# Spreading an attention stage's row scatters over its steps, one behind each step's softmax sum

## The chip, the cores and the metric

The kernel runs on one core of a Trainium2 chip. The metric is the device time of one execution in microseconds (us). The engines are named as in the profile: PE (TensorE), PEld (its weight loads), DVE (VectorE), ACT (ScalarE), POOL (GpSimd) and SP (SyncE, which here only issues DMAs). Each engine works through its own instructions in the order in which the program gives them; engines wait for each other by semaphores.

## What is computed

Three layers, one behind the other, in float32. Only what matters here stands below.

```python
def _attn_ref(q, k, v, n_global, n_local):          # q, k, v: 2 x 8 x 768 x 64
    scores = scale * np.matmul(q, k.transpose(0, 1, 3, 2)) + bias
    scores = np.where(is_global | is_local, scores, -1000000000.0)
    a = np.exp(scores - np.max(scores, axis=-1, keepdims=True))
    a = a / (np.sum(a, axis=-1, keepdims=True) + 1e-09)
    return np.matmul(a, v)

def _moe_ref(x, w_gate, w_noise, noise, w1, w2):     # x: 1536 tokens x 512, 8 experts
    noisy_logits = x @ w_gate + np.log1p(np.exp(x @ w_noise)) * noise
    top2 = np.argpartition(-noisy_logits, 2, axis=1)[:, :2]
    ...
    for e in range(E):
        ...
            h = np.maximum(x[mask] @ w1[e], 0.0)
            out[mask] += top2_w[mask, k, None] * (h @ w2[e])

def _moe2_ref(x, w_in, w_out):
    h = x @ w_in
    g = h * (1.0 / (1.0 + np.exp(-h)))
    return (g @ w_out).astype(np.float32)
```

## The kernel before, in words

The 1536 tokens are 12 tiles of 128 (6 for each batch). **The attention stage** is one loop over steps s = 0 to 50 (line 715). Step s belongs to tile n = s // 4 and to the pair of heads c = s % 4. It has a small software pipeline: `scores(s)` (line 503) is two score matmuls on PE, one for each head of the pair, and a DVE operation on each that adds the bias and takes the minimum (line 516); `expo(s)` (line 519) is the exponential of both on ACT, whose running sum goes into a column of `SM[n]` (line 526). Two steps later `p_t` transposes the result on PE into a bank of PSUM and copies it out on ACT (lines 535 and 537), three steps later `av` multiplies it with the values (line 547). So PE, DVE and ACT hand small pieces of work to each other several times in a step. Around this the loop hangs the preparation of the next tile (lines 486 to 501), the normalising of the tile before (`post`, line 554, whose row factor is the small DVE operation at line 556), loads (lines 382 to 392 on SP), and at c = 3 of tiles 2 to 7 a split of a weight block into two float32r parts on POOL (`split_high`, `split_low`, lines 317 and 324).

**Routing** (`route`, line 603) runs for groups of tiles: tiles 0 to 3, 4 to 7, 8 and 9, 10 and 11. It is a generator that the loop advances piece by piece. It finds the two experts of every token and the row that the token gets in a buffer `XS` in HBM (448 rows for each expert), and then scatters the normalised tiles there, each tile twice (j = 0 for its first expert's row, j = 1 for its second's), by an indirect DMA of 128 rows that POOL issues (line 642). By the order of the generator, the scatters of the first group are issued in step 26, those of the second in step 42, those of the third in step 50; those of the last group come in the expert stage. Between the j = 0 and the j = 1 scatters of the second group, SP's queue gets the loads of expert 0's first two blocks from `XS` (`load_x`, line 687). `reads` is the list of such loads, `scats` that of the scatters; the lists serve to tell the framework that they touch different rows.

**The expert stage** (line 1052 on) and the last layer follow. They are long chains of matmuls on PE (lines 788 to 852), with weights that stream in through SP's queue as buffers come free.

Of the kernel before, what the change touches and what calls it, by code (L numbers as in the profile page):

```python
# [9 lines left out]
F32 = mybir.dt.float32  # L10
# [10 lines left out]
P = 128  # L21
# [9 lines left out]
def fr(t):  # L31
    return t.bitcast(F32)


def noisy_logits(nc, tl, L, nz, lg, fine=False):


    co = (2.0000000078777487, 0.6666631593508026, 0.40024853723499904, 0.27961418834331303, 0.2817465726538725)
    E = lg.shape[-1]
    z = L[:, :, E:]  # L40
    a, b, s2, pl = tl("ta", E), tl("tb", E), tl("tc", E), tl("td", E)
    nc.scalar.activation(a, z, AF.Abs)
    nc.scalar.activation(a, a, AF.Tanh, scale=0.5)
    yield
    nc.vector.tensor_scalar(b, a, 3.0, None, op0=OP.add)
    nc.vector.reciprocal(b, b)
    if fine:
        yield
    nc.vector.tensor_scalar(a, b, 4.0, -1.0, op0=OP.mult, op1=OP.add)
    nc.vector.tensor_tensor(s2, a, a, op=OP.mult)  # L50
    if fine:
        yield
    nc.vector.tensor_scalar(pl, s2, co[4], None, op0=OP.mult)
    for kk in (3, 2, 1):
        nc.vector.scalar_tensor_tensor(pl, pl, co[kk], s2, op0=OP.add, op1=OP.mult)
        if fine and kk != 2:
            yield
    nc.vector.scalar_tensor_tensor(pl, pl, co[0], a, op0=OP.add, op1=OP.mult)
    yield
    nc.vector.scalar_tensor_tensor(pl, z, 0.0, pl, op0=OP.max, op1=OP.add)  # L60
    nc.vector.tensor_tensor(lg, pl, nz, op=OP.mult)
    nc.vector.tensor_tensor(lg, lg, L[:, :, :E], op=OP.add)
# [188 lines left out]
def attn_moe_mlp(ctx, tc, q, k, v, n_global, n_local, w_gate, w_noise, noise,  # L251
                 w1, w2, w_in, w_out, out):
    nc = tc.nc
# [5 lines left out]
    HP = H // 2  # L259
# [5 lines left out]
    XR = E * CAP  # L265
# [12 lines left out]
    xnp = xctx.enter_context(tc.tile_pool(name="xnp", bufs=1))  # L278

    XS = dram.tile([XR, DM], F32, name="XS")  # L280
# [40 lines left out]
    def split_low(k, pool):  # L321
        u, part = divmod(k, 2)
        hi, lo = unit[u][2 * part:2 * part + 2]
        (nc.gpsimd if pool else nc.vector).tensor_tensor(lo, raw[k], fr(hi), op=OP.subtract)  # L324
# [16 lines left out]
    slots = xnp.tile([P, NT, 2], I32, name="slots")  # L341
# [139 lines left out]
    QH, SB, PN, MN, SM, PT, OT, XT, XN = {}, {}, {}, {}, {}, {}, {}, {}, {}  # L481
# [37 lines left out]
    def expo(s):  # L519
        n, c = divmod(s, HP)  # L520
        wd = WK if tiles[n][1] else P
        if c == 0:
            SM[n] = xnp.tile([P, H], F32, name="sm", bufs=3)
        PN[s] = awk.tile([P, 2, WK], F32, name="pn", bufs=3)
        for j in range(2):
            nc.scalar.activation(PN[s][:, j, :wd], SB[s][:, j, :wd], AF.Exp, bias=MN[s][:, j:j + 1], scale=-1.0,  # L526
                                 accum_out=SM[n][:, 2 * c + j:2 * c + j + 1])
# [69 lines left out]
    T0, T1 = 8, 2  # L597
# [3 lines left out]
    scats, fills, reads = [], [], []  # L601

    def route(t0, t1, psum, fine=False):
        m = t1 - t0
        g = slice(t0, t1)

        def tl(nm, *sh):
            return xnp.tile([P, GM, *sh], F32, name=nm)[:, :m]

        lg, sel, lu, lh = lgs[:, g], sels[:, g], lus[:, g], slh[:, g]  # L610
        yield from noisy_logits(nc, tl, L[:, g], nz[:, g, :], lg, fine)
        if fine:
            yield
        top = tl("top", 8)
        for t in range(t0, t1):
            nc.vector.max(top[:, t - t0], lgs[:, t])
        nc.vector.tensor_tensor(sel, lg, top[:, :, 1:2].to_broadcast([P, m, E]), op=OP.is_ge)
        if fine:
            yield
        yield  # L620
        pos = psum()[:, :m * E].rearrange("p (t e) -> p t e", e=E)
        nc.tensor.matmul(pos, tri, sel, start=True, stop=False)
        for s in range(1, m):
            nc.tensor.matmul(pos[:, s:], ones, sel[:, :m - s], start=False, stop=False)
        nc.tensor.matmul(pos, ones, selcum[:, None, :].to_broadcast([P, m, E]), start=False, stop=True)
        un, s3 = tl("un", E), tl("s3", E)
        nc.vector.tensor_scalar(un, sel, BIG2, -BIG2, op0=OP.mult, op1=OP.add)
        if not fine:
            yield
        nc.vector.tensor_tensor(s3, pos, eover[:, None, :].to_broadcast([P, m, E]), op=OP.is_ge)  # L630
        nc.vector.scalar_tensor_tensor(s3, s3, BIG, pos, op0=OP.mult, op1=OP.add)
        if fine:
            yield
        nc.vector.tensor_tensor(lh[:, :, 0], un, s3, op=OP.subtract)
        nc.vector.tensor_tensor(lh[:, :, 1], sel, s3, op=OP.mult)
        if fine:
            yield
        nc.vector.tensor_reduce(lu, lh, axis=AX.X, op=OP.max)
        nc.vector.tensor_tensor(slots[:, g, :], lu, sgn[:, None, :].to_broadcast([P, m, 2]), op=OP.mult)
        for j in range(2):  # L640
            for t in range(t0, t1):
                st = nc.gpsimd.indirect_dma_start(
                    out=XS[:, :], out_offset=bass.IndirectOffsetOnAxis(ap=slots[:, t, j:j + 1], axis=0),
                    in_=XN[t], in_offset=None, bounds_check=XR - 1, oob_is_err=False)
                for o in scats + (reads if j else []):
                    tc.declare_no_dep(st.ins, o.ins, reason="rows of other slots")
                scats.append(st)
            if j == 0 and t1 in (T0, NT):
                for t in ((0, 1) if t1 == T0 else (2, 3)):
                    load_x(0, t)  # L650
        yield
        cs = xnp.tile([P, E], F32, name="cs")
        nc.vector.tensor_reduce(cs, sel.rearrange("p t e -> p e t"), axis=AX.X, op=OP.add)
        nc.vector.tensor_tensor(selcum, selcum, cs, op=OP.add)
        if t1 == T0:
            nc.vector.tensor_copy(chk[:, E + 1:E + 2], selcum[:, 0:1])
# [30 lines left out]
    def load_x(e, t):  # L687
        XE[e, t] = (xnp if e == 0 else mx_).tile([P, DM], F32, name="xe", bufs=4)
        a, b = blk[e][t]
        ld = (nc.gpsimd if e == 0 and t > 1 else nc.sync).dma_start(XE[e, t][:b - a], XS[e * CAP + a:e * CAP + b, :])  # L690
        reads.append(ld)

    routing, later = [], []
    R1, R2 = (0,1,1,1), (1,2,0,2)
    NS = NT * HP

    def start(g):
        if next(g, g) is not g:
            later.append(g)

    def routed(k):
        for _ in range(k):
            if routing and next(routing[0], routing) is routing:
                routing.pop(0)

    def prep(c):
        for g in prep_q(0, c, c + 2), prep_k(0, c, c + 2, c == 0):
            for _ in g:
                pass
# [5 lines left out]
    for s in range(NS + 3):  # L715
        n, c = divmod(s, HP)
        if s < NS:
            scores(s)
            expo(s)
        if s == 0:  # L720
            prep(HP // 2)
        later = [g for g in later if next(g, g) is not g]
        routed(R1[c])
        if 2 <= s < NS + 2:
            p_t(s - 2)
        if 3 <= s < NS + 3:
            av(s - 3)
        if c == 0:
            later = [g for g in later if next(g, g) is not g]
        routed(R2[c])  # L730
        if n < NT:
            if c == 0 and 2 <= n + 2 < NT:
                load_qk(n + 2)
                load_v(n + 2)
            if c == 1 and n + 1 < NT:
                start(prep_q(n + 1))
            if c == 2 and n + 1 < NT:
                start(prep_k(n + 1))
            if s == 1:
                late_consts()  # L740
            if s == 2:
                load_small()
            if s == 6:
                zero_fill()
        if c == 3 and n >= 1:
            start(post(n - 1, tbank))
        if c == 0 and n >= 2 and n - 2 in groups:
            routing.append(route(*groups[n - 2], tbank, True))
        if c == 1 and 2 <= n <= 10:
            load_half(n - 2)  # L750
        if c == 3 and 2 <= n <= 7:
            split_high(n - 2, True)
            split_low(n - 2, True)
    for g in later + routing:
        for _ in g:
            pass
# [295 lines left out]
    for i, (e, f, tm, ts) in enumerate(steps):  # L1052
# [23 lines left out]
        s = slice(blk[e][ts[0]][0], blk[e][ts[-1]][1])  # L1076
# [3 lines left out]
        n = s.stop - s.start if e < E - 1 else HC  # L1080
# [112 lines left out]
    for gr, f in todo:  # L1193
# [10 lines left out]
        if gr + 1 < len(GS):  # L1204
            t, m = tok[gr + 1], GS[gr + 1]
            a, odd = divmod(f - (G0 if gr == 0 else 2), 2)
# [39 lines left out]
```

## Time and profile before

| | |
|---|---|
| median of 3 runs | 757.39 us (755.98 to 757.83) |
| profiled execution | 757.51 us |
| its span, first to last instruction | 755.6 us |
| outside the span | 1.9 us |
| PE busy | 724.7 us (96%) |
| DVE busy | 454.1 us (60%) |
| ACT busy | 271.9 us (36%) |
| POOL busy | 192.2 us (25%) |
| mean granted TensorE clock | 0.990 |

The profile is of one execution. Times in it count from the first instruction. The attention stage fills about the first 135 us, the expert stage the stretch from there to about 500 us, the last layer the rest. In the timeline, a row is one instruction or several alike: start, duration, engine, line, operation, the tiles that it writes and reads, the form, the count; in brackets the idle time of the engine before it and who ended that. The ends of matmuls are modelled. The end of a scatter's row is the end of what POOL does for it, not the landing of its data.

### The profile page before, as it was taken

The numbers are of one execution on the slowest core, as the hardware profiler recorded it, in microseconds if no ns is written. First come the engines' busy times: TensorE is split into PE (matmuls) and PEld (weight loads), VectorE is DVE, ScalarE is ACT, GpSimd is POOL, SyncE is SP. The second block draws the span as 40 slices with busy tenths as digits, with TensorE's granted clock in tenths as the row PEclk, the third lists the DMA queues.
The fourth block names the chain that finished last, engine by engine and source line by source line (L and its number), as shares of the span: only waits on it lengthen the run. The fifth ranks groups of instructions, "written<-read, shape, count | busy, mean of one in ns | idle before, by whom it ended". The sixth has DMA issues, their size and how long they took to land.

```text
span 755.6 us, 11279 instructions
## 1 busy us (share of the span) xinstructions
PE 724.7 (96%) x4055; PEld 596.5 (79%) x4055; DVE 454.1 (60%) x991; ACT 271.9 (36%) x635; POOL 192.2 (25%) x178
## 2 busy tenths in 40 slices
PE   8997897998998999999999999999999999999996
PEld 4665565897887787888888888888888888888995
DVE  4668574747888898887888874674233332322332
ACT  5665574334343443433333454452112111111110
POOL 4134503345443333353434221422011000000000
PEclk9999997999999999999999999999999999999999
DMA  8866755258868578686868743752012010000101
GB/s 161 203 151 147 220 153 187 84 175 245 284 215 295 172 248 259 208 272 201 275 217 265 240 169 125 239 167 72 28 29 56 14 57 1 0 1 1 57 0 33
DMA packets 96431, 111.93 MB, mean 148 GB/s; under 512 B 36495, under 2 KB 65999, under 8 KB 96360
## 3 DMA queue, kind: packets, MB, share of 16 engines
q1 hardware_dynamic: 89096, 94.37, 41.7%
q0 software_dynamic: 6608, 16.10, 6.5%
q8 instruction: 43, 0.70, 0.4%
q10 hardware_dynamic: 656, 0.53, 0.2%
q14 instruction: 28, 0.23, 0.1%
HBM read 84.00 MB, written 32.51 MB: 154 GB/s over the span
## 4 chain that ended last, share of the span: by engine, by line
PE 61%; DVE 3%; issue 2%; DMA 1%; ACT 0%; POOL 0%; POOLq 0%; ACTq 0%
PE h L788 10%; PE h L789 10%; PE h L791 10%; PE y L837 9%; PE y L841 9%; PE y L842 9%; PE tp L770 2%; PE y L851 1%; PE y L852 1%; DVE ct L903 1%; DMA yu<-YS,gidx 0%; POOL co L909 0%; DMA YS<-ye 0%; DVE ct L906 0%; DVE co L908 0%
## 5 line engine op out<-in xcount | busy, mean ns | idle before, releaser
L788 PE MATMUL h<-xh,u1h 128*128 128x256 f32 (+4 forms) x544 | 181.4, 345 | 2.6 <-DVE h L1061 2.5
L789 PE MATMUL h<-xh,u1l 128*128 128x256 f32 (+4 forms) x544 | 178.1, 339 | 0.0
L841 PE MATMUL y<-u2h,hx 128*128 128x512 f32 x368 | 145.4, 395 | 1.0 <-ACT hx L814 1.0
L842 PE MATMUL y<-u2l,hx 128*128 128x512 f32 x368 | 145.1, 394 | 0.0
L1146 DVE CAST hx<-h 128x256 fp32r<-128x256 f32 (+1 forms) x64 | 35.7, 558 | 153.4 <-ACT h L1145 152.4
L791 PE MATMUL h<-xl,u1h 128*128 128x256 f32 (+4 forms) x544 | 118.2, 339 | 0.0
L837 PE MATMUL y<-u2h,hx 128*128 128x512 f32 x368 | 109.3, 396 | 6.6 <-DVE hx L815 6.6
L788 PEld LDWEIGHTS h<-xh,u1h 128*128 128x128 f32 x544 | 102.5, 188 | 14.1 <-DVE h L1061 2.9
L789 PEld LDWEIGHTS h<-xh,u1l 128*128 128x128 f32 x544 | 102.6, 189 | 10.2
L791 PEld LDWEIGHTS h<-xl,u1h 128*128 128x128 f32 x544 | 91.7, 188 | 8.2
L1145 ACT ACTIVATE h<-h 128x256 f32<-128x256 f32 (+1 forms) x64 | 30.4, 475 | 183.0 <-PE h L791 182.9
L837 PEld LDWEIGHTS y<-u2h,hx 128*128 128x128 f32 x368 | 68.8, 188 | 24.6 <-DVE hx L815 9.3
L909 POOL TENSOR_TENSOR co<-ct,co 128x512 f32<-128x512 f32 x32 | 41.3, 1289 | 167.2 <-issue 128.9
L841 PEld LDWEIGHTS y<-u2h,hx 128*128 128x128 f32 x368 | 69.2, 188 | 13.8 <-ACT hx L814 1.2
L842 PEld LDWEIGHTS y<-u2l,hx 128*128 128x128 f32 x368 | 69.2, 188 | 12.4
L1084 ACT ACTIVATE hx<-h 128x64 fp32r<-128x64 f32 x64 | 14.3, 224 | 143.1 <-DVE hx L815 143.1
L526 ACT ACTIVATE pn<-sb,mn 128x232 f32<-128x232 f32 (+1 forms) x96 | 44.8, 467 | 42.0 <-DVE mn L516 37.0
L773 DVE TENSOR_TENSOR xl<-tp,xh 128x512 fp32r<-128x512 f32 (+1 forms) x44 | 28.1, 642 | 39.5 <-ACT xh L772 39.5
L815 DVE SCALAR_TENSOR_TENSOR hx<-h,hx 128x448 fp32r<-128x448 f32 (+2 forms) x72 | 38.7, 537 | 20.7 <-ACT hx L814 19.1
L814 ACT ACTIVATE hx<-h 128x448 fp32r<-128x448 f32 (+2 forms) x72 | 34.7, 482 | 34.5 <-PE h L791 31.1
L324 POOL TENSOR_TENSOR u1l<-ra,u1h 128x1024 fp32r<-128x1024 f32 x16 | 41.4, 2587 | 6.1 <-ACT u1h L319 5.8
L319 ACT CAST u1h<-ra 128x1024 fp32r<-128x1024 f32 x37 | 38.9, 1052 | 5.4 <-DMA ra<-WI 4.1
(226 smaller groups left out, 1046.2 us busy)
## 6 DMA issues: line engine op xcount, KB each, us to landing
ra<-in_moe_w SPq DMA_DIRECT2D x32, 512.0 KB
rb<-in_moe_w SPq DMA_DIRECT2D x32, 512.0 KB
cx<-in_moe_w_in SPq DMA_DIRECT2D x16, 512.0 KB
cx<-in_moe_w_out SPq DMA_DIRECT2D x16, 512.0 KB
xe<-XS SPq DMA_DIRECT2D x22, 256.0 KB
YS<-yx SPq DMA_DIRECT2D x18, 256.0 KB
WI<-co SPq DMA_DIRECT2D x16, 256.0 KB
WO<-co SPq DMA_DIRECT2D x16, 256.0 KB
```

The costliest lines, as they stand in the source:

```text
L319: nc.scalar.copy(hi, raw[k])
L324: (nc.gpsimd if pool else nc.vector).tensor_tensor(lo, raw[k], fr(hi), op=OP.subtract)
L526: nc.scalar.activation(PN[s][:, j, :wd], SB[s][:, j, :wd], AF.Exp, bias=MN[s][:, j:j + 1], scale=-1.0, accum_out=SM[n][:, 2 * c + j:2 * c ...
L788: nc.tensor.matmul(p, a, xh[:, c, s], start=(c == 0), stop=False)
L789: nc.tensor.matmul(p, b, xh[:, c, s], start=False, stop=False)
L791: nc.tensor.matmul(p, wh[:, c, o:o + P], xl[:, c, s], start=False, stop=(c == NC - 1))
L815: nc.vector.scalar_tensor_tensor(hl, p, 0.0, fr(hh), op0=OP.max, op1=OP.subtract)
L837: nc.tensor.matmul(PY[t][:s.stop - s.start], hl[:, s], uh[:, a, :], start=False, stop=(f == nf - 1))
L841: nc.tensor.matmul(PY[t][:s.stop - s.start], hh[:, s], uh[:, a, :], start=(f == 0), stop=False)
L842: nc.tensor.matmul(PY[t][:s.stop - s.start], hh[:, s], ul[:, a, :], start=False, stop=False)
L909: nc.gpsimd.tensor_tensor(o, a, o, op=OP.add)
L1146: nc.vector.tensor_copy(hh, p)
```

## The change

In the steps of the attention stage a new function `leave(s)` is called behind `expo(s)`. If scatters are pending, it puts a copy of one column of the step's softmax sums to a one-column tile `paced` onto POOL's queue, and behind it one pending scatter. The scatters of the first group (eight: both j of tiles 0 to 3) and the j = 1 scatters of the second group (four) are put on the pending list where they were issued before; all others are issued where they were. What is pending behind the loop's end would be issued there. So the first group's scatters go to steps 27 to 34, the second group's four j = 1 scatters to steps 43 to 46, and the second group's j = 0 scatters stay four in a row in step 42.

```diff
+        def scatter(t, j):
+            st = nc.gpsimd.indirect_dma_start(
+                out=XS[:, :], out_offset=bass.IndirectOffsetOnAxis(ap=slots[:, t, j:j + 1], axis=0),
+                in_=XN[t], in_offset=None, bounds_check=XR - 1, oob_is_err=False)
+            for o in scats + (reads if j else []):
+                tc.declare_no_dep(st.ins, o.ins, reason="rows of other slots")
+            scats.append(st)
+
         for j in range(2):
             for t in range(t0, t1):
-                st = nc.gpsimd.indirect_dma_start(
-                    ...
-                scats.append(st)
+                if t1 < T0 or t1 == T0 and j:
+                    pend.append((scatter, t, j))
+                else:
+                    scatter(t, j)
...
+    pend = []
+    paced = xnp.tile([P, 1], F32, name="paced")
+
+    def leave(s):
+        n, c = divmod(s, HP)
+        if pend:
+            nc.gpsimd.tensor_copy(paced, SM[n][:, 2 * c:2 * c + 1])
+            fn, *a = pend.pop(0)
+            fn(*a)
+
...
             scores(s)
             expo(s)
+            leave(s)
...
+    for fn, *a in pend:
+        fn(*a)
```

## Rows read from the trace of the kernel before

**Rows 1.** Windows: length, busy us of each engine (count), granted clock, DMA share, GB/s.
```profile
112.20:123.70 11.50, 7.53 (x56) 4.77 (x54) 4.10 (x17) 3.29 (x12) 7.84 (x8) 0.79 0.59 203
124.00:129.60 5.60, 5.25 (x29) 3.30 (x30) 3.65 (x18) 3.67 (x13) 0.00 (x0) 0.54 0.52 192
160.00:180.00 20.00, 20.00 (x136) 17.93 (x135) 12.93 (x24) 8.55 (x16) 8.85 (x7) 1.00 0.86 265
```

**Rows 2.** Timeline, PE: first score matmul of steps 32, 35 and 36.
```profile
85.92 0.46 PE L511 MATMUL h<-kth,qh 64*128 64x232 f32 x1
...
92.83 0.46 PE L511 MATMUL h<-kth,qh 64*128 64x232 f32 x1
...
95.68 0.46 PE L511 MATMUL h<-kth,qh 64*128 64x232 f32 x1
```

**Rows 3.** Timeline, PE: first score matmul of steps 28 and 44 to 47.
```profile
72.33 0.46 PE L511 MATMUL h<-kth,qh 64*128 64x232 f32 x1
...
115.27 0.46 PE L511 MATMUL h<-kth,qh 64*128 64x232 f32 x1
...
120.55 0.75 PE L511 MATMUL h<-kth,qh 64*128 64x232 f32 x1
...
125.40 0.75 PE L511 MATMUL h<-kth,qh 64*128 64x232 f32 x1
...
128.57 0.75 PE L511 MATMUL h<-kth,qh 64*128 64x232 f32 x1
```

**Rows 4.** Timeline, POOL: scatters that begin, and within the second run, end a run.
```profile
69.88 1.25 POOL L642 DMA_INDIRECT XS<-xn,slots  x1 [1.75 <-DVE slots L639]
...
112.17 1.07 POOL L642 DMA_INDIRECT XS<-xn,slots  x1 [19.67 <-DVE slots L639]
...
116.09 0.97 POOL L642 DMA_INDIRECT XS<-xn,slots  x1 [0.31 <-issue]
...
121.20 0.97 POOL L642 DMA_INDIRECT XS<-xn,slots  x1 [0.30 <-issue]
135.73 0.97 POOL L642 DMA_INDIRECT XS<-xn,slots  x1 [13.55 <-DVE slots L639]
...
147.74 0.97 POOL L642 DMA_INDIRECT XS<-xn,slots  x1 [7.20 <-DVE hx L815]
```

**Rows 5.** Timeline: what PE finished inside the runs of eight, and its readers.
```profile
115.86 0.70 PE L535 MATMUL tp<-ident,pn 128*116 128x128 f32 x4
119.41 0.40 DVE L516 CUSTOM_DVE_ANT_0 sb<-y,bias 128x232 f32<-128x232 f32 x1 [0.91 <-remote]
...
123.71 0.58 ACT L537 COPY pts<-tp 116x512 f32<-116x512 f32 x1 [3.27 <-PE y L535]
...
81.66 0.60 ACT L489 ACTIVATE qh<-y 128x512 f32<-128x512 f32 x1 [1.06 <-PE y L547]
```

**Rows 6.** Timeline: PE and its reader ACT beside a run of four, beside two scatters.
```profile
138.37 0.61 PE L791 MATMUL h<-xl,u1h 128*128 128x192 f32 x4
...
140.04 0.33 ACT L814 ACTIVATE hx<-h 128x192 fp32r<-128x192 f32 x1 [0.83 <-PE h L791]
...
147.79 0.61 PE L791 MATMUL h<-xl,u1h 128*128 128x192 f32 x4
...
148.49 0.33 ACT L814 ACTIVATE hx<-h 128x192 fp32r<-128x192 f32 x1 [0.51 <-PE h L791]
```

**Rows 7.** Timeline: a POOL split, and small DVE work beside it and beside a scatter.
```profile
64.66 1.05 POOL L317 TENSOR_SCALAR u2h<-rb 128x1024 fp32r<-128x1024 f32 x1 [6.88 <-DMA rb<-in_moe_w]
65.79 2.35 POOL L324 TENSOR_TENSOR u2l<-rb,u2h 128x1024 fp32r<-128x1024 f32 x1
65.99 2.18 DVE L627 TENSOR_SCALAR un<-sels 128x32 f32<-128x32 bf16 x1
...
70.29 0.68 DVE L498 COPY kth<-tp 128x512 f32<-128x512 f32 x1
```

**Rows 8.** Timeline, ACT: the exponential of step 44's first head.
```profile
118.54 0.49 ACT L526 ACTIVATE pn<-sb,mn 128x232 f32<-128x232 f32 x1 [3.34 <-DVE mn L516]
```

More of the change, by code (lines that the diff above doesn't have):

```diff
@@ L639, in route @@
         nc.vector.tensor_tensor(slots[:, g, :], lu, sgn[:, None, :].to_broadcast([P, m, 2]), op=OP.mult)
+        def scatter(t, j):
[5 more added lines that the diff above has]
+            scats.append(st)
         for j in range(2):
             for t in range(t0, t1):
-                st = nc.gpsimd.indirect_dma_start(
[L643 to L646, printed above, removed]
-                scats.append(st)
+                if t1 < T0 or t1 == T0 and j:
+                    pend.append((scatter, t, j))
+                else:
+                    scatter(t, j)
             if j == 0 and t1 in (T0, NT):
```

## The prediction, made before the changed kernel was run

> **What bounds the kernel now.** I read first which engine is busy in which stretch, then the steps of the attention stage by their first score matmul, then what POOL, ACT and DVE do where a step is long. In the expert stage PE is busy for 20.00 of 20 us [rows 1]: what starts earlier there ends earlier. In the attention stage no engine is full; a step lasts as long as its round of handovers PE to DVE to ACT to PE. An undisturbed tile of four steps takes 95.68 - 85.92 = 9.76 us, and its first three steps 92.83 - 85.92 = 6.91 us [rows 2]. Two stretches are far longer. Steps 28 to 31 take from 72.33 to 85.92, 13.59 us, 3.83 more than an undisturbed tile; steps 44 to 46 take from 115.27 to 128.57, 13.30 us, 6.39 more than the same three steps undisturbed [rows 2, 3]. Together 10.22 us: the ceiling of what a change there can bring.
>
> Both stretches lie on a run of eight scatters on POOL. The first begins at 69.88, the second at 112.17, and its last begins at 121.20, so one scatter comes every (121.20 - 112.17) / 7 = 1.29 us [rows 4]. What is late in them is not an engine's work but the news of PE's work. PE ends a transpose at 115.86 + 0.70 = 116.56, and ACT, idle for 3.27 us by then, starts to read it only at 123.71; DVE gets the second half of a score matmul of step 44 at 119.41, some 3.5 us after PE made it [rows 5]. While everybody waits, PE is busy for 7.53 of 11.50 us and its granted clock falls, to a mean of 0.79 there and 0.54 in 124 to 129.6, which is mostly the lower of its two levels, 1.2 GHz [rows 1].
>
> When does it clear? In the second run (123.71 - 112.17) / 8 = 1.44 us for each scatter after the run's begin, in the first, where ACT's copy of the queries comes free at 81.66, (81.66 - 69.88) / 8 = 1.47 us [rows 4, 5]. The 119.41 is 5 x 1.45 us behind the begin. In a run of four that begins at 135.73 PE ends at 138.37 + 0.61 = 138.98 and ACT starts at 140.04, 1.06 us later, which is 3 x 1.44 us behind the begin [rows 4, 6]. Beside two scatters only, the first at 147.74, PE ends at 148.40 while that scatter is under way, and ACT starts at 148.49, 0.09 us later [rows 4, 6]. So I read it as a queue: each scatter costs some 1.44 us (an estimate) in something that PE's signals must pass, scatters come every 1.29 us, and once two or three stand in it, PE's signals stand behind them. Spaced by more than 1.44 us they should hold up nothing.
>
> **The first eight scatters.** They leave in steps 27 to 34, whose length is about 2.4 us, more than 1.44. But POOL also has two weight splits in its queue, behind the scatters of steps 27 and 31, and a split waits for its weights: one of before waited 6.88 us, then took 1.05 and 2.35 us [rows 7]. So behind the first split the scatters of steps 28 to 31 have gathered, whose sums are there already, and they go as a run of up to four, each with a copy between; behind the second split a run of up to three. The price of such a run lies between nothing and the 1.06 us of the run of four [rows 6]; I take 0.3, since the copy stretches the spacing towards 1.44 us. Of the 3.83 us 3.5 come back: **-3.5 us**, bounds -2.8 and -3.8.
>
> **The second group.** Its first four scatters stay, from 112.17 on, so nothing changes until the last of them, which starts at 116.09 and ends at 117.06 [rows 4]. By the queue's rule their 4 x 1.44 us end at 117.93. The fifth waits for step 43's sum, which is long there, so it follows at once: the queue then ends at 119.37. The sixth waits for step 44's sum. ACT makes it from 118.54 to 119.03 [rows 8], so this scatter can't come before 119.1, when the queue is empty, and the two behind it wait for steps 45 and 46. Step 45 then starts at 120.55 as before [rows 3], but its results are not held up. PE has been idle by then and may be at the lower clock. With two steps at what a step at the lower clock took, 128.57 - 125.40 = 3.17 us [rows 3], step 47 starts at 126.9, 1.7 us earlier than before; with two undisturbed ones (6.91 / 3 = 2.3 us) at 125.2, 3.4 us earlier; if the fifth scatter is no burden, all is released some 1.44 us earlier still, 4.8 us. I take the middle: **-3.2 us**, bounds -1.7 and -4.8.
>
> **The rest.** The twelve copies of one column are work for POOL alone, somewhere between nothing and the 1.05 us of a whole split's first half [rows 7], nearest to nothing by their size; POOL has nothing that the attention stage waits for, so they cost nothing, and a few tenths each if a run on POOL came to be waited for. Behind POOL's new waits stand the two splits, which the expert stage needs some 50 us later, and the scatters themselves. Whom do late scatters hold up? A tile's buffer comes round eight tiles later, in step 36 at the earliest, two steps after the last pending scatter of the first group; the loads from `XS` on SP's queue wait for the same j = 0 scatters as before, whose place hasn't moved. If that cover were gone, DVE would wait for a landing. The splits themselves move in time, and a split's second half can hold a small DVE operation: the one of 2.35 us held the operation at line 627 for 2.18 us [rows 7]. For each of two splits that is 0 to +2.2 us; a tile has one such small operation (line 556) on the path, so I take 0 and keep +2.2 once for the range. Everything behind the attention stage moves up as a whole; shifted collisions there I bound by the same +-2.2 us.
>
> **The sum.** -3.5 - 3.2 = -6.7 us, on the profiled execution's own 757.51 us, which is 0.12 us above the median of the runs shown: **750.8 us**.
>
> **Rivals.** *Every scatter holds PE's signals, alone or not* (the slower end). The place is each of the twelve steps that get one, the price that of the late handover beside the run of four, 1.06 us [rows 6]: 12 x 1.06 = 12.7 us in place of the 10.2 that are lost now, +2.5 us, 760.0 us. It is slower than before from 10.2 / 12 = 0.85 us for each scatter on. For it speaks that the attention's steps hand over far more often than the expert stage, where I saw two scatters go by harmlessly; against it those 0.09 us [rows 6]. Chance 0.10.
>
> *POOL shuts DVE out while it works on a scatter.* Then each costs DVE about its 0.97 us wherever it stands, 12 x 0.97 = 11.6 us before and after, and nothing changes: 757.5 us. Against it: DVE's copy from 70.29 to 70.97 ran inside the scatter from 69.88 to 71.13, and ACT was late as well [rows 4, 5, 7]. The Trainium skill speaks for this rival (SBUF — State Buffer, section "SBUF: two separate sides"): VectorE in its two-port modes and GpSimd share a port pair under an exclusive lock, and the loser waits for the whole instruction. The trace agrees for a split, 2.18 us at line 627 [rows 7], and not for that scatter. Chance of no change, for this or another reason, 0.13.
>
> *Only the first group gains.* The fifth scatter follows the four at once and the sixth 1.5 us later; if the queue doesn't empty in between, the second group stays a run of six or more and gains at most the 0.5 us that two waits give: 757.5 - 3.5 = 754.0 us. That the change doesn't part what it means to part there is the weakest place of the forecast. Chance 0.17.
>
> *Both stretches become undisturbed*: 757.5 - 10.2 = 747.3 us, if even the run of four in step 42 costs nothing. The late signal of 119.41 speaks against it, since by the queue's rule four scatters suffice for some of it. Chance 0.05.
>
> **How the numbers follow.** The forecast, 747.5 to 753, has the remaining 0.55. About 0.3%, 2.3 us, is what a measurement of this kernel can tell from no change. Faster by more than that (under 755.1): 0.55 + 0.05 + 0.17 = 0.77; the same 0.13; slower 0.10. The range takes in the forecast, the case of the first group alone, the ceiling with half a microsecond to spare and the lower half of the no-change case, and leaves out the slower case, the upper half and little below: 746.5 to 757.5.
>
> **What would show it.** In the trace of the changed kernel the first-group scatters stand singly or in runs of up to four behind a split; steps 28 to 31 take 9.8 to 10.5 us; PE's transposes are read by ACT within a few tenths; a sixth scatter of the second group starts behind 119 us and steps 44 to 46 take 8.5 to 11.6 us; the granted clock dips once, around 119 to 124 us, not around 82. The expert stage starts 6 to 7 us earlier. I would be wrong if steps with a single scatter were each longer than those of [rows 2], if ACT were still late beside spaced scatters, or if the small operation at line 556 took 2 us beside a split.

## The result, and the profile after

The changed kernel takes 750.83 us (median of 4 runs, 749.24 to 751.67), the kernel before, beside it on the same chip, 757.28 us (4 runs, 755.98 to 757.83). The ratio is 0.9915, with a 95% interval of 0.9894 to 0.9936: 6.45 us or 0.85% faster. The profiled execution of the changed kernel took 750.52 us, its span is 748.7 us, its mean granted clock 0.994.

The page's totals come first: span, then busy time, share and number of instructions of each engine. No engine has less to do (POOL has 12 instructions and 2.5 us more), so what went is waiting.

```profile
span 748.7 us, 11295 instructions
PE 724.5 (97%) x4055; PEld 596.8 (80%) x4055; DVE 453.1 (61%) x991; ACT 272.0 (36%) x635; POOL 194.7 (26%) x190
```

Where it went is read from the first score matmuls of the steps, as in [rows 2, 3]. The table adds them up; the last column is the kernel before once more, on a chip where no handover is late (e1 in the experiments below).

| stretch, us | before | after | before, where nothing is late |
|---|---|---|---|
| start of step 28 | 72.33 | 71.33 | 68.75 |
| steps 28 to 31 | 13.59 | 9.05 | 9.05 |
| steps 32 to 39 | 19.52 | 21.14 | 19.50 |
| steps 40 to 43 | 9.83 | 9.83 | 9.83 |
| steps 44 to 46 | 13.30 | 10.65 | 5.88 |
| step 47 to the end of the span | 627.0 | 626.7 | 628.4 |

From before to after the span shrinks by 6.9 us: 4.54 in steps 28 to 31, less 1.62 that comes back in steps 32 to 39, 2.65 in steps 44 to 46, 1.0 ahead of step 28 and 0.3 behind step 47.

POOL's timeline of the changed kernel (start, duration, line, tiles, in brackets the idle time before and who ended it) shows the new order. First the stretch of the first group:

```profile
72.18 1.25 POOL L641 DMA_INDIRECT XS<-xn,slots  x1 [0.76 <-DVE rs L557]
73.86 1.04 POOL L317 TENSOR_SCALAR u1h<-ra 128x1024 fp32r<-128x1024 f32 x1 [0.43 <-DMA ra<-in_moe_w]
...
77.64 1.07 POOL L641 DMA_INDIRECT XS<-xn,slots  x1 [0.16 <-issue]
78.72 0.19 POOL L706 COPY paced<-sm 128x1 f32<-128x1 f32 x1
...
81.76 0.98 POOL L641 DMA_INDIRECT XS<-xn,slots  x1 [0.16 <-issue]
```

One scatter stands alone, a split of weights follows, and four scatters have gathered behind it, a copy of 0.19 us ahead of each; a second split and a run of three follow. Then the second group:

```profile
108.25 0.98 POOL L641 DMA_INDIRECT XS<-xn,slots  x1 [16.55 <-DVE slots L639]
...
112.10 0.98 POOL L641 DMA_INDIRECT XS<-xn,slots  x1 [0.30 <-issue]
...
113.43 0.99 POOL L641 DMA_INDIRECT XS<-xn,slots  x1 [0.16 <-issue]
...
116.01 0.98 POOL L641 DMA_INDIRECT XS<-xn,slots  x1 [0.55 <-issue]
118.08 0.18 POOL L706 COPY paced<-sm 128x1 f32<-128x1 f32 x1 [1.09 <-ACT pn L526]
```

The fifth follows the four at once, the sixth comes 2.6 us behind it, and the copies make the others wait for their step's sum. The handovers there, in the timelines of PE, DVE and ACT:

```profile
111.35 0.46 PE L511 MATMUL h<-kth,qh 64*128 64x232 f32 x1
111.94 0.70 PE L535 MATMUL tp<-ident,pn 128*116 128x128 f32 x4
...
114.06 0.40 DVE L516 CUSTOM_DVE_ANT_0 sb<-h,bias 128x232 f32<-128x232 f32 x1 [3.19 <-PE y L547]
...
115.59 0.56 ACT L537 COPY pts<-tp 116x512 f32<-116x512 f32 x1
115.65 0.74 PE L511 MATMUL h<-kth,qh 64*128 64x232 f32 x1
...
118.82 0.75 PE L511 MATMUL h<-kth,qh 64*128 64x232 f32 x1
...
122.00 0.70 PE L511 MATMUL h<-kth,qh 64*128 64x232 f32 x1
```

Step 44 is still late, 4.30 us: its first scores are made from 111.35 on and DVE reads them at 114.06. But that is the end of it. ACT copies the transposes out at 115.59, 2.95 us behind PE's end at 112.64, and it comes to them straight from its exponentials, without a wait; before it was 7.15 us, the last 3.27 of them idle [rows 5]. Steps 45 and 46 take 3.17 and 3.18 us, with matmuls of 0.75 us in place of 0.46. The windows (length, busy us of PE, PEld, DVE, ACT and POOL with counts, granted clock, DMA share, GB/s) show why:

```profile
68.20:80.40 12.20, 10.86 (x94) 7.03 (x93) 9.07 (x35) 7.61 (x29) 8.43 (x10) 1.00 0.71 174
108.25:119.75 11.50, 9.32 (x69) 5.99 (x66) 6.30 (x26) 5.60 (x20) 7.39 (x10) 0.82 0.53 175
115.60:119.00 3.40, 3.40 (x19) 2.12 (x20) 1.76 (x8) 2.16 (x9) 1.36 (x3) 0.51 0.57 145
119.00:123.40 4.40, 4.40 (x24) 2.78 (x24) 3.04 (x14) 1.80 (x7) 1.97 (x3) 0.60 0.93 338
123.40:129.00 5.60, 5.60 (x64) 4.33 (x63) 4.48 (x25) 2.68 (x8) 0.00 (x0) 1.00 0.14 53
```

PE, idle for part of step 44 (busy for 9.32 of the 11.50 us around it), has a granted clock of 0.51 from 115.6 to 119.0 and of 0.60 from there to 123.4, that is mostly 1.2 GHz, and is back at 2.4 GHz behind that. The first group has no such dip.

### The profile page after: what moved, and what is told of

It is laid out like the page before. It is cut to its first block, busy times and chain, and to the rows that moved or that the text cites. A ratio compares the mean times of both kernels' runs of the same rounds, so it can differ in the third digit from the quotient of the medians.

```text
span 748.7 us, 11295 instructions
## 1 busy us (share of the span) xinstructions
PE 724.5 (97%) x4055; PEld 596.8 (80%) x4055; DVE 453.1 (61%) x991; ACT 272.0 (36%) x635; POOL 194.7 (26%) x190
## 3 DMA queue, kind: packets, MB, share of 16 engines
q0 software_dynamic: 6608, 16.10, 6.6%
## 4 chain that ended last, share of the span: by engine, by line
PE 81%; DVE 9%; issue 5%; DMA 2%; ACT 1%; POOL 1%; another core or an unknown queue 0%; SPq 0%; POOLq 0%; ACTq 0%; DVEq 0%
PE h L808 11%; PE h L809 11%; PE h L811 11%; PE y L857 10%; PE y L861 10%; PE y L862 10%; PE h L511 4%; PE y L547 3%; PE tp L535 3%; PE tp L790 2%; DVE ct L923 2%; PE y L535 1%; PE y L871 1%; PE y L872 1%; PE tp L496 1%
## 5 line engine op out<-in xcount | busy, mean ns | idle before, releaser
L809 PEld LDWEIGHTS h<-xh,u1l 128*128 128x128 f32 x544 | 102.6, 189 | 10.2
```

The lines of the kernel that those rows point to most:

```text
L809: nc.tensor.matmul(p, b, xh[:, c, s], start=False, stop=False)
```

## The experiments

The theory under test is the queue: scatters close behind each other hold up the news of PE's work, and scatters spaced by more than some 1.44 us (the forecast's estimate) don't. Its rivals are that every scatter holds it up, that POOL's work itself does (by shutting DVE out, or in another way), that the rows' data do, and that the wait for the step's sum is what helps, not the spacing. The chips are given by their number in the run's record; the number of the chip of the first measurement isn't recorded. Each numbered chip was used at one time only, so that a chip and the time can't be told apart, and the steps of the kernel before are known from the first measurement and from chip 14 alone. In the diffs and names, L641, L642 and L512 are the same scatter and score lines as above, shifted by added lines.

| kernel | chip | us | before there, us | ratio (95%) | steps 28 to 31 / 32 to 39 / 44 to 46, us |
|---|---|---|---|---|---|
| e1, before | 14 | 743.16 | 744.67 | one run | 9.05 / 19.50 / 5.88 |
| e2, gap | 14 | 744.49 | 744.67 | 0.9993 (0.9959 to 1.0026) | 9.05 / 19.50 / 5.87 |
| e3, no wait | 14 | 743.86 | 744.67 | 1.0003 (0.9971 to 1.0034) | 9.05 / 19.50 / 5.88 |
| e4, dropped rows | 14 | 743.46 | 744.67 | 0.9981 (0.9961 to 1.0001) | 9.05 / 19.49 / 5.88 |
| e11, first group only | 8 | 744.49 | 744.51 | 1.0006 (0.9980 to 1.0033) | 9.05 / 19.49 / 5.87 |
| e12, second group only | 8 | 744.38 | 744.51 | 1.0001 (0.9970 to 1.0032) | 9.05 / 19.50 / 5.87 |
| e10, gap behind all | 8 | 745.84 | 744.51 | 1.0010 (0.9978 to 1.0042) | 9.05 / 19.50 / 5.88 |
| e5, the change | 5 | 751.25 | 759.15 | 0.9894 (0.9839 to 0.9948) | 9.04 / 24.33 / 11.05 |
| e6, gap | 5 | 748.13 | 759.15 | 0.9873 (0.9813 to 0.9933) | 9.05 / 19.50 / 5.88 |
| e7, dropped rows | 0 | 765.60 | 759.12 | 1.0112 (1.0037 to 1.0188) | 15.93 / 19.96 / 14.92 |
| e8, no wait | 0 | 754.48 | 759.12 | 0.9963 (0.9931 to 0.9996) | 9.04 / 21.13 / 13.35 |
| e9, smaller gap | 0 | 751.74 | 759.12 | 0.9910 (0.9883 to 0.9936) | 9.76 / 20.40 / 8.18 |

**The kernel before, once more (e1).** No edit.

> The kernel before, unchanged, profiled once more. Every theory: about 757.4 us, steps 28 to 31 in about 13.6 us and steps 44 to 46 in about 13.3 us again. Open is what it shows of steps 18 to 27, which took 24.3 us in the first trace of before and 24.4 us less 1.0 to 2.1 us in the changed kernel's without any edit there: if they differ between two executions of the same kernel by a microsecond, that part of the gain is chance; if they agree within 0.2 us, the change reaches back there.

On chip 14 the kernel before takes 743.16 us, and 744.67 us is its median over 25 runs there: 12.6 us less than at the first measurement. Its timelines of POOL, PE and ACT:

```profile
104.04 1.07 POOL L642 DMA_INDIRECT XS<-xn,slots  x1 [18.28 <-DVE slots L639]
...
107.13 0.46 PE L511 MATMUL h<-kth,qh 64*128 64x232 f32 x1
107.72 0.70 PE L535 MATMUL tp<-ident,pn 128*116 128x128 f32 x4
109.34 0.56 ACT L537 COPY pts<-tp 116x512 f32<-116x512 f32 x1
...
113.01 0.46 PE L511 MATMUL h<-kth,qh 64*128 64x232 f32 x1
113.07 0.97 POOL L642 DMA_INDIRECT XS<-xn,slots  x1 [0.30 <-issue]
```

The same eight scatters, 1.29 us apart, and nothing is late: ACT reads the transposes 0.92 us behind their end at 108.42, and steps 44 to 46 take 113.01 - 107.13 = 5.88 us. The two stretches of before are 4.54 + 0.02 + 7.42 = 12.0 us longer than here, about the whole difference of the medians. So the scatters' order alone doesn't make news late; it takes something more, which went with the chip. This is a condition that neither the forecast nor its rivals had. The expectation's 24.3 us for steps 18 to 27 was misread: they take 26.44 us in the first trace and 24.44 here, so two executions of one kernel, on two chips, differ there by 2.0 us.

The traces also hold the times at which PE's semaphore was counted up, which none of the rows above shows. In e1, from 40 to 140 us, every count comes within 0.05 us of the modelled end of its matmul. In the kernel before the same holds from 40 to 66 us and from 95 to 104, away from the scatters. But in the second stretch the transposes that end at 116.56 are counted at 123.63, 0.08 us ahead of ACT's copy, and what ended before them, the two halves of the scores at 115.93 among it, at 116.48, 117.92, 117.97 and 119.39, in PE's order. So it is the count itself that is late; neither a slow reader nor an engine ahead of the reader makes up the 7.15 us.

**A gap behind each scatter (e2 on chip 14, e6 on chip 5).** The order stays that of before, eight in a row; a memset on POOL of a 128x512 tile that nothing else touches spaces them:

```diff
                 scats.append(st)
+                if t1 <= T0:
+                    nc.gpsimd.memset(gap, 0.0)
```

> The kernel before with one edit: behind each scatter of the first two groups GpSimd writes zeros to an unused 128 x 512 tile, so that the scatters of a run start some 1.6 to 1.8 us apart and not 1.29 us; nothing waits for a step's sums and the runs stay eight long. Queue theory (each scatter holds PE's signals for about 1.44 us, lateness only where they come closer): no lateness in either run, most of the ceiling of 10 us, 747 to 750 us. Lock theory (POOL shuts DVE out while it works on a scatter): more POOL work, no gain, 757 to 760 us. If the length of the run counts and not its spacing: 756 to 758 us.

> The kernel before with zeros written on GpSimd behind each scatter of the first two groups, so that they start some 1.6 to 1.8 us apart; once more, since the first time fell on a chip without any late handover. Where before takes 756 to 758 us: queue theory 745 to 748 us (about as on a quiet chip), lock theory 757 us or more, length of the run theory 756 to 758 us. Where before takes 742 to 746 us: the same as before, as the first time.

On chip 14 there is nothing to gain: 0.9993. On chip 5 it is 0.9873 of before and has the lowest median of that chip, 748.13 us (745 to 748 were expected) beside 751.25 us for the change (e5, below). The two intervals overlap, but the steps tell them apart: all three stretches of e6 are undisturbed. POOL, PE and ACT in e6:

```profile
106.79 1.07 POOL L642 DMA_INDIRECT XS<-xn,slots  x1 [16.54 <-DVE slots L639]
107.86 0.55 POOL L649 MEMSET gap<- 128x512 f32 x1
108.58 0.98 POOL L642 DMA_INDIRECT XS<-xn,slots  x1 [0.17 <-issue]
...
109.89 0.46 PE L511 MATMUL h<-kth,qh 64*128 64x232 f32 x1
110.48 0.70 PE L535 MATMUL tp<-ident,pn 128*116 128x128 f32 x4
112.09 0.56 ACT L537 COPY pts<-tp 116x512 f32<-116x512 f32 x1
115.77 0.46 PE L511 MATMUL h<-kth,qh 64*128 64x232 f32 x1
118.64 0.97 POOL L642 DMA_INDIRECT XS<-xn,slots  x1 [0.17 <-issue]
```

The scatters of the second group come every (118.64 - 108.58) / 6 = 1.68 us, all eight in a row, and steps 44 to 46 take 115.77 - 109.89 = 5.88 us, as on chip 14; ACT reads the transposes 0.91 us behind their end. A spaced scatter isn't quite without effect: a count of PE's for an end at 109.37 comes at 109.91, 0.54 us late, but no step is longer for it. POOL has more to do than before, so it isn't POOL's work that holds the others up, nor each scatter by itself, and the wait for the sums isn't needed.

**The change without its wait (e3 on chip 14, e8 on chip 0).** The scatters keep their places in the changed kernel's program:

```diff
         if pend:
-            nc.gpsimd.tensor_copy(paced, SM[n][:, 2 * c:2 * c + 1])
             fn, *a = pend.pop(0)
```

> The changed kernel without the copy of the step's sum: the scatters keep their places in the program, but GpSimd waits for no step. Queue theory: the second group runs as eight in a row again at 1.29 us and loses about what it gained, 2.7 us; the first group still has its weight splits between its scatters, so it keeps most of its gain: 752.5 to 755 us. If only the wait for the sums matters: 757 us, as before. If the places in the program alone do it: 750 to 751.5 us.

> The changed kernel without the copy of the step's sum, so that GpSimd waits for no step; once more, for the same reason. Where before takes 755 to 762 us: by the queue theory the second group runs eight in a row at 1.29 us again (steps 44 to 46 in 13 us against 10.7 to 11.0 with the wait), the first group keeps its weight splits between the scatters: 752.5 to 756 us; if the wait for the sums is all, as before, 757 to 760 us; if the places in the program are all, as the changed kernel, 750 to 752.5 us.

On chip 14 again nothing (1.0003). On chip 0 the two groups part. In the first nothing is lost against the first measurement of the change: 9.04 and 21.13 us beside 9.05 and 21.14 with the wait (on chip 5, in e5, it is 24.33 with the wait). POOL's two splits part these scatters by themselves, into one, four and three. The second group is back where it was, 13.35 us beside 13.30 before:

```profile
106.64 0.97 POOL L641 DMA_INDIRECT XS<-xn,slots  x1 [16.67 <-DVE slots L639]
...
109.74 0.46 PE L511 MATMUL h<-kth,qh 64*128 64x232 f32 x1
...
115.60 0.98 POOL L641 DMA_INDIRECT XS<-xn,slots  x1 [0.30 <-issue]
118.23 0.59 ACT L537 COPY pts<-tp 116x512 f32<-116x512 f32 x1 [2.76 <-PE y L535]
...
123.09 0.75 PE L511 MATMUL h<-kth,qh 64*128 64x232 f32 x1
```

POOL runs ahead and issues all eight, (115.60 - 106.64) / 7 = 1.28 us apart. ACT gets the transposes at 118.23, which is 8 x 1.45 us behind the first scatter. So, as far as single traces of different chips show it, the wait earns what it earns in the second group alone, and as spacing.

**Scatters whose rows are dropped (e4 on chip 14, e7 on chip 0).** To the changed kernel come eight scatters in step 26 and four behind the four of step 42. They go to a buffer that nobody reads, with a bound of 1 that drops nearly every row, so that they are scatters with next to no data (POOL's DMA queue moves 16.11 MB with them and 16.10 without; twelve that write would add 3.1 MB):

```diff
+        def dropped(t, j):
+            st = nc.gpsimd.indirect_dma_start(
+                out=XD[:, :], out_offset=bass.IndirectOffsetOnAxis(ap=slots[:, t, j:j + 1], axis=0),
+                in_=XN[t], in_offset=None, bounds_check=1, oob_is_err=False)
...
+                    dropped(t, j)
```

> The changed kernel with twelve scatters added whose rows are all but dropped by their bound and which move next to no data (to a buffer nobody reads): eight in a row in step 26, and four behind the four of step 42, where the kernel before had its runs. If a scatter's work on POOL and its descriptors make the queue: both stretches are long again, 757 to 761 us. If the rows' data on the DMA engines make it: as the changed kernel, 750 to 752.5 us.

> The changed kernel with twelve scatters added whose rows are all but dropped by their bound (to a buffer nobody reads), eight in a row in step 26 and four behind the four of step 42; once more, since the first time fell on a chip without late handovers. Where before takes 755 to 762 us: if a scatter's work on POOL and its descriptors hold PE's signals, the run in step 26 makes steps 27 to 30 long and the one in step 42 makes steps 44 to 46 take 13 us, 755 to 762 us in all; if the rows' data hold them, as the changed kernel, 750 to 753 us. Where before takes 742 to 746 us: nothing to see, the same as before.

On chip 14 a dozen more scatters change nothing (0.9981). On chip 0 they make the kernel 1.12% slower than before, 3.6 us above the range that was expected, and hold PE's news as scatters with data do. POOL, PE and ACT in e7:

```profile
80.49 0.99 POOL L642 DMA_INDIRECT XS<-xn,slots  x1 [0.16 <-issue]
...
83.16 0.60 ACT L490 ACTIVATE qh<-y 128x512 f32<-128x512 f32 x1 [2.49 <-PE y L512]
...
114.98 0.98 POOL L642 DMA_INDIRECT XS<-xn,slots  x1 [16.57 <-DVE slots L640]
...
118.67 0.70 PE L536 MATMUL tp<-ident,pn 128*116 128x128 f32 x4
...
120.11 0.98 POOL L650 DMA_INDIRECT XD<-xn,slots  x1 [0.30 <-issue]
...
126.55 0.59 ACT L538 COPY pts<-tp 116x512 f32<-116x512 f32 x1 [2.59 <-PE y L536]
```

ACT reads the transposes 126.55 - 119.37 = 7.18 us late, as before (7.15 us), and that is (126.55 - 114.98) / 8 = 1.45 us for each scatter behind the run's begin, although half of them carry next to nothing. In the first stretch eight dropped scatters begin at 69.90, and a ninth, which writes, follows them at 80.49. Steps 28 to 31 take 15.93 us there, more than beside eight that write (13.59 us), but ACT's copy of the queries comes free at 83.16, (83.16 - 69.90) / 9 = 1.47 us for each of nine, as before for each of eight. The data of the rows are not the cause. The four dropped scatters of the second group began after PE had ended at 119.37 and yet delayed its news, so this isn't one queue served in the order of coming, as the forecast took it. Nor does all news wait for the last scatter: DVE reads step 44's scores at 120.90 and 122.94, and the transposes' news comes at 126.55 although a ninth scatter began at 125.31. What decides is not shown.

**A smaller gap (e9, chip 0).** As e6, with a memset of half the size:

```diff
-    gap = xnp.tile([P, DM], F32, name="gap")
+    gap = xnp.tile([P, 256], F32, name="gap")
```

> The kernel before with zeros written on GpSimd behind each scatter of the first two groups as in the run with the gap, but only to a 128 x 256 tile: the scatters start some 1.45 us apart instead of 1.69 us. The queue's service time was estimated as 1.44 us for each scatter. Where before takes 755 to 762 us: if it is that, nearly no lateness and 747 to 750 us, as with the wide gap; if it is nearer to 1.69 us, part of the steps are long, 751 to 756 us.

It takes 751.74 us, 0.9910 of before: the gain of the change, though its stretches are not free. POOL, PE and DVE:

```profile
72.48 0.99 POOL L642 DMA_INDIRECT XS<-xn,slots  x1 [0.18 <-issue]
...
77.75 0.44 PE L547 MATMUL y<-pts,vt 128*64 128x128 f32 x4
...
78.70 0.46 PE L511 MATMUL h<-kth,qh 64*128 64x232 f32 x1
...
79.85 0.69 DVE L551 COPY xt<-y 128x512 f32<-128x512 f32 x1 [1.80 <-PE y L511]
...
81.28 0.97 POOL L642 DMA_INDIRECT XS<-xn,slots  x1 [0.17 <-issue]
82.25 0.46 PE L511 MATMUL h<-kth,qh 64*128 64x232 f32 x1
```

The spacing is (81.28 - 72.48) / 6 = 1.467 us. Steps 28 to 30 take 78.70 - 72.49 = 6.21 us (72.49 is step 28's first score matmul), as in e1. Step 31 is the first long one, 3.55 us: DVE waits 1.80 us, until 79.85, for the attention output that PE had finished at 77.75 + 0.44 = 78.19, behind the fifth scatter, and only then comes to the scores of the step. Step 32 (3.00 us) has another reason beside late news: DVE's small operation at line 556 takes 1.80 us there, from 81.83 on, beside a memset and the first half of a split on POOL. At 1.29 us it goes faster: in the changed kernel the scores of 111.35 come late behind three scatters, from 108.25 to 110.82, and beside a fourth. So a spacing of 1.467 us is not enough here and 1.68 us is on chip 5; the estimate of 1.44 us was somewhat low. It is the spacing and not an instruction between the scatters that counts, since the smaller memset stands there too.

**The change, once more (e5, chip 5).** No edit to the changed kernel.

> The changed kernel, unchanged, beside the kernel before. On the chip of the runs so far of this study (before 744.67 us) no handover of PE was late in any trace, with eight or with sixteen scatters in a row, and no spacing changed the time. If the lateness belongs to the chip, or to its state, and not to the kernel: where before takes 742 to 746 us, the changed kernel takes the same within 1.5 us; where before takes 756 to 758 us, the changed kernel takes 6 to 7 us less. If the change has a worth of its own besides the lateness, it is faster on a quiet chip too, 740 to 742 us; if the copies and waits cost something, 746 us or more there.

It gains again, 0.9894, or 7.9 us where 6 to 7 were expected. But the place differs. POOL and PE:

```profile
77.26 1.07 POOL L641 DMA_INDIRECT XS<-xn,slots  x1 [0.17 <-issue]
...
78.98 0.46 PE L511 MATMUL h<-kth,qh 64*128 64x232 f32 x1
...
81.39 0.98 POOL L641 DMA_INDIRECT XS<-xn,slots  x1 [0.16 <-issue]
...
83.37 0.75 PE L511 MATMUL h<-kth,qh 64*128 64x232 f32 x1
...
87.60 0.75 PE L511 MATMUL h<-kth,qh 64*128 64x232 f32 x1
```

The run of four behind the split, which cost 0.84 us in step 32 of the first profile (2.95 us for 2.11), here makes steps 32 and 33 last 4.39 and 4.23 us and brings the lower clock, seen in matmuls of 0.75 us; steps 32 to 39 take 4.83 us more than undisturbed. So the same run in the same program costs 0.8 or some 5 us. It begins 78.98 - 77.26 = 1.72 us ahead of step 32's scores here and 2.74 us ahead of them in the first profile (77.64, scores at 80.38), and the chip is another; which of the two counts isn't settled.

**Each half of the change alone (e11, e12), and a gap behind every scatter (e10), all on chip 8.**

e11 is the changed kernel with the first group's scatters alone on the pending list, e12 with the second group's alone, e10 is e2 without its condition:

```diff
-                if t1 < T0 or t1 == T0 and j:
+                if t1 < T0:
```

```diff
-                if t1 < T0 or t1 == T0 and j:
+                if t1 == T0 and j:
```

```diff
                 scats.append(st)
+                nc.gpsimd.memset(gap, 0.0)
```

> Half of the change: only the first group's eight scatters leave one in a step; the second group runs eight in a row as before. Where before takes 755 to 762 us: steps 28 to 31 in about 9.1 us but one or two of steps 32 to 36 longer by 0.8 to 2.3 us, since four scatters gather behind the first weight split; steps 44 to 46 in about 13.3 us. 2 to 3.5 us less than before. Where before takes 742 to 746 us: the same.

> The other half: only the second group's four j = 1 scatters leave one in a step; the first group runs eight in a row as before. Where before takes 755 to 762 us: steps 28 to 31 in about 13.6 us, steps 44 to 46 in 10.7 to 11.0 us instead of 13.3. 2 to 3.5 us less than before, and with the other half's gain together what the whole change gives. Where before takes 742 to 746 us: the same.

> The kernel before with zeros written on GpSimd to a 128 x 512 tile behind every scatter, those of the third and last group too (1.69 us apart in the run with the gap). Where before takes 755 to 762 us: queue theory, all steps undisturbed and the one late handover beside the run of four (about 1 us) gone too, 746 to 748.5 us; if the third group's POOL work is waited for, 749 to 751 us. Where before takes 742 to 746 us: the same as before.

Chip 8 is like chip 14: before takes 744.51 us there, the three stretches are undisturbed in all three kernels, and the ratios are 1.0006, 1.0001 and 1.0010. These runs say nothing on the halves, nor on the third and fourth group's scatters; they say that a memset of 0.55 us behind each scatter costs nothing that can be measured. What each half is worth on a chip with late news rests on the sums of steps alone.

## Why the prediction was right, and where by luck

Predicted were 750.8 us, measured 750.83 us. The mechanism was right in the main: scatters close behind each other hold up PE's news. Its picture of how, a queue served in order, was not, and three of its sizes were off, and they met.

- **The ceiling.** The step that failed is the yardstick: the tile of [rows 2] was taken for undisturbed for every tile. Steps of other tiles are shorter, 9.05 and 5.88 us where nothing is late. The ceiling was 12.0 us, not 10.2.
- **The first eight scatters,** forecast -3.5, measured -2.92 us. Steps 28 to 31 came out at 9.05 us, better than the 9.8 to 10.5 that were named, but the runs behind the splits cost 2.95 and 2.90 us in steps 32 and 36, where undisturbed steps take 2.11: 1.63 us in place of 0.3. Its upper bound for one such run, 1.06 us from [rows 6], was no bound, as e5 shows with 4.83 us for steps 32 to 39: in the attention stage a late handover can bring the lower clock as well. And these scatters owe their parting to the splits, not to the sums (e8).
- **The second group,** forecast -3.2, measured -2.65 us. The queue served in order was the wrong picture: in the kernel before the transposes ended at 116.56, behind four scatters, and yet cleared behind the eighth (1.44 us for each of eight, in the forecast's own rows), and DVE got the first scores there at 118.10, 5.93 us behind the begin, much as here, where it got them at 114.06, 5.81 us behind it. Here the transposes' count came at 115.43, (115.43 - 108.25) / 5 = 1.44 us for each of five, so the fifth scatter did hold it, but ACT was at its exponentials until then and lost nothing. Step 44 became 0.98 us shorter (4.30 for 5.28) and step 45 1.68 us (3.17 for 4.85); step 46 stayed at 3.18, at the lower clock, the dearer of the two prices that the forecast weighed.
- **What made up for it.** The two terms give -5.6 us, and the span shrank by 6.9. The 1.0 us ahead of step 28 is no gain of the change: steps 18 to 27 took 26.44 us before, 24.38 in the changed kernel and 24.44 in e1, which is the kernel before, but 25.38 in e5, which is the changed one. Single executions differ by that much there.
- **The rest.** The twelve copies cost nothing that can be measured, as e4 (0.9981), e11 (1.0006) and e12 (1.0001) say, which have all or part of them; the clock dips once, from some 115.6 to 122.5 us (named were 119 to 124, with the second run's begin at 112.17 in place of 108.25); the expert stage starts earlier and is as long as before (626.7 and 627.0 us).
- **The rivals.** *Every scatter holds PE's signals* falls as a price with e6, eight scatters in a row and no step longer. *POOL shuts DVE out* falls too, for scatters: in e6 POOL does more and no step is longer, and in e1 the same scatters of 0.97 us stand beside the same DVE work without a loss. (The DVE copy that the forecast held against it reads PSUM. In the kernel before a better case is DVE's operation of line 654 at 114.12, which has two inputs in SBUF: it takes 0.17 us inside the scatter from 113.55 on, where a small operation beside a split took 2.18 us [rows 7].) *Only the first group gains* was wrong where the news is late, since the sixth scatter did come behind its step's sum; e8, which lacks the wait, is what that rival described. *Both stretches undisturbed* is what e6 reaches and the change doesn't.
- **What no case held.** On the two numbered chips 8 and 14 nothing is late in any trace, and neither the change's halves (e11, e12), nor its order without the wait (e3), nor the whole of it with dropped scatters added (e4) gains or loses there. The forecast's price went with the chip, and nothing in one profile says so.

Open: why PE's news is late on some chips and not on others (the traces with late news also lack some of the semaphore counts: they keep 7515 to 7702 in all, those of chips 8 and 14 8055 to 8235); by what rule the news is let through; which part of a scatter, POOL's 0.97 us of work or what the DMA engines then do with its 128 descriptors, takes the 1.45 us; and whether the gap of 1.68 us would gain behind the later scatters on a chip with late news.

## What to carry to other kernels

Where a reader on another engine starts microseconds behind its producer's end with nothing of its own to do, look for indirect DMAs that GpSimd issues back to back, and space them by about 1.7 us (1.68 was enough here, 1.47 was not), with other work or a small memset; a wait for something that comes once in a step does the same only if steps are that long and nothing ahead in the queue lets the scatters gather. Take the undisturbed length of a step from the same steps of an undisturbed execution, not from a neighbouring tile. And time such a change on more than one chip: the same pair of kernels differed by 0.85%, by 1.06% and, as its halves and e4 show for other chips, by nothing.

## What the runs showed of the hardware that was not expected

- The kernel before takes 744.5 to 744.7 us on chips 8 and 14 and 757.3 to 759.2 us on chips 0, 5 and that of the first measurement, each used at one time. Where before was traced, almost all of the difference is PE's late news in two stretches of the attention stage (12.0 of 12.6 us for the first measurement against chip 14).
- What is late is the count of PE's semaphore: 7.07 us behind the end of step 44's transposes in the kernel before, at most 0.05 us behind any matmul's end in e1's attention stage from 40 us on.
- A run of eight scatters 1.28 to 1.29 us apart releases the news of step 44's transposes 1.44 to 1.45 us for each scatter behind its begin (before, e7, e8), whether all rows are written or half of the scatters drop theirs. The three runs begin in the same phase of the step, so they are one case seen three times; the first run gives 1.47 us, with eight (before) and with nine (e7).
- Scatters that begin after PE's work has ended still delay its news (e7: four of them, from 120.11 on, for an end at 119.37).
